# First batch's input on all 128 partitions, a three-product first step, and later raw weights in a Fourier filter with two MLPs

## The chip, the cores and the metric

One core of one Trainium2 chip. TensorE (PE; PEld is its weight load) multiplies, VectorE (DVE), ScalarE (ACT) and GpSimd (POOL) do elementwise work, SyncE (SP) issues most DMAs. The metric is device microseconds (us) of one launch; less is better.

## The reference

```
X = rfft(x, axis=1)                       # x: 2 x 3008 x 256
y = irfft(X * (filt_r + 1j*filt_i)[None], n=3008, axis=1)
t = y.reshape(6016, 256)
h = t @ w_in;  t = (h * sigmoid(h)) @ w_out            # d_ff 2048
g = t @ w_gate; t = (g*sigmoid(g) * (t @ w_val)) @ w_out2   # d_ff 1536
```

All in float32. The kernel makes exact enough products out of pairs of float32r parts (high and low), three products each.

## The kernel before, in words

3008 is 64 x 47, and the transform is done as two short ones by matrix products with constant matrices: step 1 along 47 (padded to 48; two sequences of 48 lie on 96 partitions), step 2 along 64, the filter, step 3 back along 64, step 4 back along 47. The class `Fft` holds one batch (F0, F1).

The fill (lines 1085 to 1230) is written out by hand. F0 is done in full float32. `load_x` brings `x` in eight tiles of 96 partitions x 8 pairs x 128 values; `s1_turned` (line 244) makes four products per four pairs with the `x` values as weights and 96 columns of the constants as the moving side, so that the result is turned, and ACT or DVE copies it into `sc`. `turn` transposes it back, `s2` multiplies by the step 2 matrix and by the filter (`fr`, real part, 64 partitions loaded and `prep_f` writes the negated copy to the other 64; `fi`, imaginary part), `s3` goes back, `store_z` writes to DRAM. `load_zt` reads it back in another layout for `s4`, whose result is split into high and low parts `xh` (ACT, line 377) and `xl` (DVE, line 378): the tokens of the first MLP. `warm` issues products on zeros ahead of the first data. `load_w` brings raw weights, `conv_0` to `conv_c` rework them ("i1" is w_in, "o1" is w_out of the first MLP, in quarters and halves).

From line 1232 on a list of `units` sets the order: one unit is six products of `m1_in` for one token tile and one 128-row group of the hidden layer, and six of `m1_out` of three units earlier. A unit index at which a side task is issued stands in `at(i, ...)`: F1's steps 1 to 4 (in float32r parts), weight conversion, and the `s4` of token tiles 2 to 7 (lines 979 to 984). Units 0 to 31 hold tiles 0 and 1 together, tile 2 begins at unit 32, tile 3 at 48, and so on. All PSUM tiles come from one pool of eight banks; units 0 to 31 keep four of them as accumulators of `m1_out`, and the other four go round among `m1_in`, `s4` and F1's steps. Each engine works its instructions off in the order in which they are written, and SP and ACT issue DMAs in that order too.

Of the kernel before, what the change touches and what calls it, by code (L numbers as in the profile page):

```python
# [14 lines left out]
ALU = mybir.AluOpType  # L15
# [6 lines left out]
N, N1, N2 = 3008, 64, 47  # L22
# [6 lines left out]
P = 128  # L29
# [18 lines left out]


GROUP = 8 * N2  # L50
FW = 576
K4 = ((0, 0, 141), (94, 141, 188), (235, 329, 141))


# [4 lines left out]
def _constants():  # L59

    n1 = np.arange(N1)
    n2 = np.arange(N2)
    k2 = np.arange(SLOT)
    a1 = 2 * np.pi * U1 / N1 * np.outer(n1, n1)
    a2 = 2 * np.pi * V2 / N2 * np.outer(n2, k2)

    c1 = np.zeros((2, NP2, 2, 2, SLOT))
    for p in range(2):
        c1[p, :N2, p, 0] = np.cos(a2)
        c1[p, :N2, p, 1] = -np.sin(a2)  # L70
# [12 lines left out]
    c2[:, 1, 1] = -np.cos(a1)

    c3 = np.zeros((2, N1, N1, 2))
    c3[0, :, :, 0] = np.cos(a1)
    c3[0, :, :, 1] = np.sin(a1)
    c3[1, :, :, 0] = -np.sin(a1)
    c3[1, :, :, 1] = np.cos(a1)
    c3 /= N1  # L90

    k = (E1 * n1[:, None] + E2 * k2[None, :]) % N
    up = k > N // 2
    freq = np.where(up, N - k, k)
    sign = np.where(up, -1.0, 1.0).reshape(N1, 3, 2, 4).transpose(2, 0, 1, 3).reshape(P, 12)
    pack = np.zeros((P, FW + 512), np.float32)
    pack[:96, 0:96] = c1.reshape(96, 96)
    pack[:, 128:256] = c2.reshape(P, P)
    pack[:, 256:384] = c3.reshape(P, P)
    pack[:, 384:396] = sign  # L100
    pack[:, 448:576] = np.eye(P)
    whole = np.kron(np.eye(4), c4.reshape(96, 94))
    for t, (col, o, n) in enumerate(K4):
        pack[:, FW + o:FW + o + n] = whole[P * t:P * t + P, col:col + n]
    return pack, freq
# [6 lines left out]
def fft_filter_mlp_kernel(  # L112
# [13 lines left out]
    nc = tc.nc  # L126
# [35 lines left out]
    c4 = cp.tile([P, 512], F32, name="c4")  # L162
    cst = yp.tile([P, FW], F32, name="cst", bufs=1)

    C1, C2, C3 = (96, 0, 96), (P, 128, 256), (P, 256, 384)
    sgn = cst[:, 384:396]
    eye = cst[:, 448:576]
    csp = yp.tile([P, 2, 384], F32R, name="csp", bufs=1)

    def psum(name):  # L170
# [2 lines left out]
    def mid(shape, name, dtype=F32):  # L173
        return mp.tile(shape, dtype, tag="mid", name=name)
# [11 lines left out]
    PARTS = ((0, 0), (0, 1), (1, 0))  # L186

    def split_consts():
        nc.scalar.copy(csp[:, 0], cst[:, :384])
        nc.vector.tensor_tensor(csp[:, 1], cst[:, :384], csp[:, 0], op=ALU.subtract)  # L190

    def transform(o, m, x):

        k, c0, c1 = m
        if not isinstance(x, tuple):
            nc.tensor.matmul(o, cst[:k, c0:c1], x, start=True, stop=True)
            return
        for i, (mp_, xp_) in enumerate(PARTS):
            nc.tensor.matmul(o, csp[:k, mp_, c0:c1], x[xp_], start=(i == 0), stop=(i == 2))  # L199

    def cut(x, i, j):
        return tuple(v[:, i:j] for v in x) if isinstance(x, tuple) else x[:, i:j]

    class Fft:
# [4 lines left out]
            self.b = b  # L209
            self.xa, self.a, self.ft, self.tin, self.ys, self.zs = {}, {}, {}, {}, {}, {}  # L210

        def load_x(self, i, k=0, n=8):
            if k == 0:
                self.xa[i] = mid([96, 8, P], "x")
            j = 8 * (i % 4) + k
            nc.sync.dma_start(self.xa[i][:, k:k + n], xp[self.b, i // 4, :, j:j + n, :])

        def split(self, x, shape):
            h, l = mid(shape, "fh", F32R), mid(shape, "fl", F32R)
# [24 lines left out]
        def s1_turned(self, i, sc, part=(0, 1)):  # L244

            x = self.xa[i]
            for k in part:
                ps = psum("s1")
                for j in range(4):
                    nc.tensor.matmul(  # L250
                        ps[:, 96 * j:96 * (j + 1)], x[:, 4 * k + j, :], cst[:96, 0:96],
                        start=True, stop=True,
                    )
                m = 32 * (i % 4) + 16 * k
                dst, src = sc[:, :, m:m + 16], ps[:, :384].rearrange("p (m s) -> p s m", s=SLOT)
                if k and i < 4:
                    nc.vector.tensor_copy(dst, src)
                else:
                    nc.scalar.copy(dst, src)
# [15 lines left out]
        def load_f(self, q):  # L275
            self.ft[q] = mid([P, 8, P], "fr"), mid([P, 4, P], "fi")
            f, g = self.ft[q]
            nc.sync.dma_start(f[:64], fr[q])
            nc.sync.dma_start(g, fi[q])

        def prep_f(self, q, part):
            f, o = self.ft[q][0], 4 * part
            nc.scalar.mul(f[64:, o:o + 4], f[:64, o:o + 4], -1.0)

        def prep_g(self, q):
            g, k = self.ft[q][1], 4 * (q % 3)
# [15 lines left out]
        def s2(self, h):  # L302
            q, o = h // 2, 4 * (h % 2)
            (f, g), x = self.ft[q], self.tin[q]
            bps = psum("s2")
            bv = bps.rearrange("p (s d) -> p s d", s=4)
            transform(bv, C2, cut(x, o, o + 4))
            y = yp.tile([P, 4, P], F32, tag="y", name="y")
            t2 = t2t[h % 2]
            nc.vector.tensor_tensor(y, bv, f[:, o:o + 4], op=ALU.mult)  # L310
            for src, dst in ((0, 64), (64, 0)):
                nc.vector.tensor_tensor(  # L312
                    t2[dst:dst + 64], bv[src:src + 64], g[16 * o:16 * o + 64], op=ALU.mult
                )
# [13 lines left out]
        def s3(self, h):  # L328
            q, o = h // 2, 4 * (h % 2)
            y = self.ys.pop(h)  # L330
            zps = psum("s3")
            zv = zps.rearrange("p (s d) -> p s d", s=4)
            transform(zv, C3, y)
            if o == 0:
                self.zs[q] = mid([P, 8, P], "z")
            nc.scalar.copy(self.zs[q][:, o:o + 4], zv)

        def store_z(self, q, o=0, n=8):
            s = 8 * (q % 3) + o
# [48 lines left out]
    def load_w(key, q, half):  # L388


        src = SRC[key]
        raw = mid([P, 512, 2], "raw", U32)
        raws[key, q, half] = raw
        if key in ("o1", "o2"):
            r0 = 512 * q + 256 * half
            nc.sync.dma_start(
                raw.rearrange("p (f d) w -> p f (d w)", f=2),
                src[r0:r0 + 256, :].rearrange("(f p) d -> p f d", p=P),
            )
# [548 lines left out]
    begin = {}  # L948
# [4 lines left out]
    def at(i, fn, *args):  # L953
        todo.setdefault(i, []).append((fn, args))
# [19 lines left out]
    groups, done = [], 0  # L974
# [2 lines left out]
        groups.append([(c, g) for c in range(done, end) for g in range(2)])  # L977
        done = end
    for t in range(2, NSTD):
        i = begin[1, t] - 2 * len(groups[t])  # L980
        for k, (c, g) in enumerate(groups[t]):
            if c % 2 == 0 and g == 0:
                at(i + 2 * k - 5, load_zt, c // 2)
            at(i + 2 * k, s4, c, g)
    def weights2(i, key, q):

        for half in range(2):
# [11 lines left out]
    for b in range(len(WIDE)):  # L999
        i = len(units) + 32 * b  # L1000
# [78 lines left out]
    at(79, fft_s.close)  # L1079
    at(80, room)  # L1080

    WARM = 18
    LAG = 4
    with tc.manual_schedule():
        F0.load_x(0, 0, 4)
        nc.sync.dma_start(cst[:, 0:96], consts[:, 0:96])
        F0.load_x(0, 4, 4)
        nc.vector.memset(idle, 0.0)
        first = stp.tile([P, 512], U32, tag="m", name="m", bufs=4).bitcast(F32)
        nc.vector.memset(first[:, :1], 0.0)  # L1090
        nc.scalar.activation(first[:, :1], first[:, :1], AF.Silu)
        warm(WARM)
        for i in range(1, 4):
            F0.load_x(i)
        nc.sync.dma_start(cst[:, 96:], consts[:, 96:FW])
        F0.load_f(0)
        F0.load_x(4)
        F0.load_f(1)
        F0.load_x(5)
        F0.load_x(6)  # L1100
        F0.load_f(2)
        F0.load_x(7)
        F0.load_f(3)
        nc.sync.dma_start(c4, consts[:, FW:])
        for half in range(2):
            load_w("i1", 0, half)
        for q in range(4, 6):
            F0.load_f(q)
        F1.load_x(0)
        for half in range(2):  # L1110
            load_w("o1", 0, half)
        sc0 = zp.tile([P, SLOT, P], F32, name="sc0")
        sc1 = zp.tile([P, SLOT, P], F32, name="sc1")

# [18 lines left out]

# [169 lines left out]
```

## Time and profile before

| | us |
|---|---|
| three timed runs | 1165.92, 1166.58 (median), 1171.66 |
| the profiled execution | 1170.64 |
| its span | 1168.9 |
| PE busy | 1152.2 (99%) |
| DVE, ACT, POOL busy | 740.1, 670.2, 541.0 |

The profile is of one execution; "idle" is time in which an engine had nothing running, with the one that ended it behind an arrow. The granted clock of TensorE is given as a share of 2.4 GHz, so 0.50 is 1.2 GHz.

### The profile page before, as it was taken

How to read it: one execution, taken by the hardware profiler on the slowest of the kernel's cores; microseconds unless marked ns; L12 is line 12 of the kernel's file. 1: busy time of each engine (PE TensorE's matmuls, PEld its weight loads, DVE VectorE, ACT ScalarE, POOL GpSimd, SP SyncE). 2: the span in 40 equal slices, each digit the busy share in tenths (PEclk: the TensorE clock that was granted, in tenths of full speed). 3: DMA queues.
4: the chain of work that ended last, by engine and by line, in shares of the span. 5: the costliest groups of instructions: out<-in, count | busy, mean ns of one | idle time of the engine just before them, and what ended most of it. 6: DMA issues, size and time to landing. Idle time of an engine off the chain costs nothing.

```text
span 1168.9 us, 16228 instructions
## 1 busy us (share of the span) xinstructions
PE 1152.2 (99%) x6014; PEld 985.9 (84%) x6014; DVE 740.1 (63%) x935; ACT 670.2 (57%) x1095; POOL 541.0 (46%) x370
## 2 busy tenths in 40 slices
PE   9899899999999999999999999999999999999998
PEld 7478688888888888888998888888888888888998
DVE  4678847777666456435356676566666566667555
ACT  4678656667777675656556445445444545444543
POOL 2456624674666466644354343353353353343332
PEclk9999899999999999999999999999999999999999
DMA  9872622443545542511733612412412412413300
GB/s 213 270 230 75 157 75 78 143 136 122 171 164 182 174 165 73 171 54 37 235 116 140 225 41 87 144 55 73 161 41 88 144 56 90 133 49 103 129 17 32
DMA packets 66575, 141.73 MB, mean 121 GB/s; under 512 B 5472, under 2 KB 31072, under 8 KB 66496
## 3 DMA queue, kind: packets, MB, share of 16 engines
q1 hardware_dynamic: 66064, 140.30, 37.1%
q8 instruction: 47, 0.77, 0.3%
q10 hardware_dynamic: 432, 0.39, 0.1%
q14 instruction: 32, 0.26, 0.1%
HBM read 100.56 MB, written 40.11 MB: 120 GB/s over the span
## 4 chain that ended last, share of the span: by engine, by line
PE 75%; issue 1%; DVE 1%; POOL 0%; ACT 0%; DMA 0%; POOLq 0%; ACTq 0%; SPq 0%; DVEq 0%
PE acc L917 17%; PE y L716 15%; PE xa L716 10%; PE xb L716 10%; PE acc L615 8%; PE h L571 7%; PE acc L638 7%; PE s L362 1%; DMA wst<-ds_g 0%; POOL y L316 0%; POOLq L1296 0%; PE s L199 0%; DVE t2t L312 0%; POOL wst L511 0%; DVE xo L690 0%
## 5 line engine op out<-in xcount | busy, mean ns | idle before, releaser
L917 PE MATMUL acc<-w,h 128*128 128x256 f32 x1692 | 433.8, 279 | 0.1
L917 PEld LDWEIGHTS acc<-w,h 128*128 128x128 f32 x1692 | 314.7, 188 | 8.0 <-POOL h L875 0.3
L742 POOL TENSOR_TENSOR s<-s 128x512 f32<-128x512 f32 (+1 forms) x88 | 113.7, 1292 | 265.4 <-ACT s L741 245.4
L615 PE MATMUL acc<-h,w 128*128 128x512 f32 x768 | 200.1, 391 | 0.6 <-DVE h L579 0.6
L579 DVE TENSOR_TENSOR h<-u,h 128x512 fp32r<-128x512 f32 x128 | 135.3, 1063 | 96.8 <-ACT h L578 85.3
L716 PE MATMUL xa<-xo,w 128*128 128x512 f32 (+1 forms) x528 | 193.0, 386 | 0.0
L716 PE MATMUL y<-xo,wst 128*128 128x512 f32 (+1 forms) x528 | 191.0, 387 | 0.1
L716 PE MATMUL xb<-xo,wst 128*128 128x512 f32 (+1 forms) x528 | 190.1, 386 | 0.0
L571 PE MATMUL h<-xh,w 128*128 128x512 f32 x512 | 181.5, 396 | 5.5 <-DVE xl L378 4.9
L615 PEld LDWEIGHTS acc<-h,w 128*128 128x128 f32 x768 | 144.7, 189 | 32.5 <-DVE h L579 2.3
L638 PE MATMUL acc<-h,w 128*128 128x512 f32 (+1 forms) x384 | 138.2, 378 | 0.0
L761 DVE TENSOR_TENSOR c<-y,s 128x512 f32<-128x512 f32 (+1 forms) x88 | 59.5, 676 | 115.6 <-PE y L716 115.6
L900 POOL TENSOR_TENSOR h<-c,h 128x1024 fp32r<-128x1024 f32 (+1 forms) x35 | 83.1, 2373 | 104.4 <-ACT h L899 104.4
L571 PEld LDWEIGHTS h<-xh,w 128*128 128x128 f32 x512 | 96.6, 189 | 26.2 <-DVE xl L378 5.4
L716 PEld LDWEIGHTS y<-xo,wst 128*128 128x128 f32 x528 | 98.9, 187 | 19.0 <-DVE u L748 0.5
L716 PEld LDWEIGHTS xb<-xo,wst 128*128 128x128 f32 x528 | 99.0, 187 | 18.5
L716 PEld LDWEIGHTS xa<-xo,w 128*128 128x128 f32 x528 | 99.0, 188 | 13.8
L598 ACT ACTIVATE u<-h 128x512 f32<-128x512 f32 x128 | 76.2, 596 | 53.9 <-PE h L571 53.4
L571 PE MATMUL h<-xl,w 128*128 128x512 f32 x256 | 100.5, 392 | 0.0
L716 PE MATMUL y<-xo,w 128*128 128x512 f32 (+1 forms) x264 | 97.9, 387 | 0.4 <-DVE c L757 0.4
L872 ACT CAST h<-ga 128x1024 fp32r<-128x1024 f32 (+1 forms) x36 | 37.2, 1034 | 100.9 <-DVE ga L870 100.9
L752 DVE TENSOR_TENSOR xb<-xb,u 128x512 f32<-128x512 f32 (+1 forms) x88 | 60.0, 682 | 43.9 <-PE xb L716 43.9
(122 smaller groups left out, 1829.1 us busy)
## 6 DMA issues: line engine op xcount, KB each, us to landing
wst<-ds_g SPq DMA_DIRECT2D x36, 512.0 KB, 3.5
wst<-ds_v SPq DMA_DIRECT2D x36, 512.0 KB, 3.7
wst<-ds SPq DMA_DIRECT2D x16, 512.0 KB, 4.8
raw<-in_w_out_dram SPq DMA_DIRECT2D x14, 512.0 KB, 5.8
zt<-d SPq DMA_DIRECT2D x16, 384.0 KB, 5.8
x<-in_xp_dram SPq DMA_DIRECT2D x15, 384.0 KB, 9.3
d<-z SPq DMA_DIRECT2D x11, 512.0 KB, 3.9
d<-x SPq DMA_DIRECT2D x20, 256.0 KB, 2.8
```

Source lines behind the costliest of these rows:

```text
L571: nc.tensor.matmul(ps[:, :n], wt[key, f // 4, g][:, wpart, o:o + P], x[xpart][:, g, :n], start=(g == 0 and k == 0), stop=(g == 1 and k == 2),)
L579: nc.vector.tensor_tensor(h[:, 1, :n], u[:, :n], h[:, 0, :n], op=ALU.subtract)
L598: nc.scalar.activation(u[:, :n], ps[:, :n], AF.Silu)
L615: nc.tensor.matmul(a[:, :n], w[:, wpart, o:o + 128], h[:, xpart, :n], start=(f == 0 and k == 0), stop=(f == 15 and k == 2),)
L638: nc.tensor.matmul(a, w[:, wpart, o:o + 128], h[xpart][:, n * l:n * l + n], start=(f == 0 and k == 0), stop=(end and k == 1), skip_group_c ...
L716: nc.tensor.matmul(o, w(wpart), x[:, xpart, :o.shape[-1]], start=(first and k == 0), stop=(last and k == 2), skip_group_check=True,)
L742: nc.gpsimd.tensor_tensor(s[:, 1], s[:, 1], s[:, 0], op=ALU.add)
L752: nc.vector.tensor_tensor(self.b, self.b, self.u2, op=ALU.add)
L761: nc.vector.tensor_tensor(self.c[:, :self.n], self.y, self.s[:, 0], op=ALU.add)
L872: nc.scalar.copy(h[0], a[:, :m])
L900: nc.gpsimd.tensor_tensor(h[1], c, h[0], op=ALU.subtract)
L917: nc.tensor.matmul(a[:, D * (i % 2):D * (i % 2) + D], h[hpart][:, P * i:P * i + P], w[:, wpart, f % 2], start=(at_ == 0 and k == 0 and i % ...
```

## The change

Five things change. (1) F0's `x` tiles are laid out over 128 partitions: of four pairs, the first three stay on 96 partitions, and the fourth is cut into three pieces of 32 rows which go to partitions 96 to 127 beside them (`load_full`). `s1_turned` makes three products per four pairs: two with 144 columns and one with 192, against constants packed to fit; the order of pairs that results is undone by a permuted step 2 matrix (C2T). The 32-row pieces are issued from ACT for tiles 0 to 3 and from SP for tiles 4 to 7. (2) `load_f` loads the first half of `fr` to partitions 0 to 63 and the second half to 64 to 127, two DMAs of 64 rows instead of one; signs follow in `sgn` and in `s3`. (3) The constants come in other pieces: 288 columns first, 320 next, 256 behind `fr`, `fi` of group 1; `c4` comes behind F1's first `x`. (4) The raw weights of `o1` are loaded behind the third store of `z` instead of in the prologue, and `warm` takes 16 products instead of 18. (5) The `s4` calls of tiles 2 to 7 stand at other units: 6, 5, 3 and 2 units ahead of the tile (before: 8, 6, 4, 2), or 5 and 3 where there are two (before: 4, 2).

```diff
-FW = 576
+FW = 896
+ORDER = (0, 3, 2, 1)
...
     def split_consts():
-        nc.scalar.copy(csp[:, 0], cst[:, :384])
-        nc.vector.tensor_tensor(csp[:, 1], cst[:, :384], csp[:, 0], op=ALU.subtract)
+        for i, c, n in ((0, 144, 96), (P, 320, 2 * P)):
+            h, v = csp[:, 0, i:i + n], cst[:, c:c + n]
+            nc.scalar.copy(h, v)
+            nc.vector.tensor_tensor(csp[:, 1, i:i + n], v, h, op=ALU.subtract)
...
+        def load_full(self, i, part=(0, 1), eng=nc.sync):
+
+            if part[0] == 0:
+                self.xa[i] = mid([P, 2, 3, P], "x")
+            x, a, n = self.xa[i], part[0], len(part)
+            j = 8 * (i % 4) + 4 * a
+            src = xp[self.b, i // 4]
+            nc.sync.dma_start(
+                x[:96, a:a + n], src[:, j:j + 4 * n].rearrange("k (a t) e -> k a t e", t=4)[:, :, :3]
+            )
+            for k in part:
+                eng.dma_start(
+                    x[96:, k],
+                    src[:, 8 * (i % 4) + 4 * k + 3].rearrange("(t r) e -> r t e", r=32),
+                )
...
-                for j in range(4):
+                whole = ps[:, 96:480].rearrange("p (b c) -> p b c", c=192)[:, :, :96]
+                both = cst[:, :288].rearrange("p (b c) -> p b c", c=144)[:, :, :96]
+                for n, o, v in (
+                    (0, ps[:, :144], cst[:, 144:288]), (2, ps[:, 144:288], cst[:, 96:240]),
+                    (1, whole, both),
+                ):
                     nc.tensor.matmul(
-                        ps[:, 96 * j:96 * (j + 1)], x[:, 4 * k + j, :], cst[:96, 0:96],
-                        start=True, stop=True,
+                        o, x[:, k, n], v, start=(n == 0), stop=(n == 1), skip_group_check=True
                     )
...
-            nc.sync.dma_start(f[:64], fr[q])
+            for o in range(2):
+                nc.sync.dma_start(f[64 * o:64 * o + 64, 4 * o:4 * o + 4], fr[q][:, 4 * o:4 * o + 4])
             nc.sync.dma_start(g, fi[q])
...
-        i = begin[1, t] - 2 * len(groups[t])
-        for k, (c, g) in enumerate(groups[t]):
+        for n, (c, g) in zip((-6, -5, -3, -2) if len(groups[t]) == 4 else (-5, -3), groups[t]):
             if c % 2 == 0 and g == 0:
-                at(i + 2 * k - 5, load_zt, c // 2)
-            at(i + 2 * k, s4, c, g)
+                at(begin[1, t] + n - 5, load_zt, c // 2)
+            at(begin[1, t] + n, s4, c, g)
...
-    WARM = 18
+    WARM = 16
...
-        nc.sync.dma_start(c4, consts[:, FW:])
...
         F1.load_x(0)
-        for half in range(2):
-            load_w("o1", 0, half)
+        nc.sync.dma_start(c4, consts[:, FW:])
...
                 elif h == 5:
+                    for half in range(2):
+                        load_w("o1", 0, half)
                     for j in range(2):
                         load_zt(j, (0,))
```

SP, in the fill, where the three stores of `z` of F0's first half stand (`d_0_86<-z`), before: the raw weights of `o1` (`in_w_out`) stand ahead of them.

```order
L216 DMA x<-in_xp_dram 96x1024
L396 DMA raw<-in_w_out_dram 128x2x512 x2
L340 DMA d_0_86<-z 128x1024
L216 DMA x<-in_xp_dram 96x1024
L340 DMA d_0_86<-z 128x1024
L216 DMA x<-in_xp_dram 96x1024
L340 DMA d_0_86<-z 128x1024
L353 DMA zt<-d_0_86 128x6x128 x2
```

SP at the same place, of the changed kernel.

```order
L224 DMA x<-in_xp_dram 96x1024
L1141 DMA c_132<-in_consts_dram 128x512
L372 DMA d_0_86<-z 128x1024
L224 DMA x<-in_xp_dram 96x1024
L372 DMA d_0_86<-z 128x1024
L224 DMA x<-in_xp_dram 96x1024
L372 DMA d_0_86<-z 128x1024
L428 DMA raw<-in_w_out_dram 128x2x512 x2
L385 DMA zt<-d_0_86 128x6x128 x2
```

The two raw loads moved from ahead of the first store to between the third store and the read back, and the 256 KB of `c4` took their old place.

PE at the first `s4` of tile 2, before (unit 24; `s_1317` is its PSUM tile, `s_1347` that of F1's step 1 in unit 25).

```order
L362 MATMUL s_1317<-c_132,zt 128x141
L362 MATMUL s_1317<-c_132,zt 128x188
L362 MATMUL s_1317<-c_132,zt 128x141
L571 MATMUL h_1327<-xh,w 128x512
L571 MATMUL h_1327<-xl,w 128x512
L571 MATMUL h_1327<-xh,w 128x512 x2
L571 MATMUL h_1327<-xl,w 128x512
L571 MATMUL h_1327<-xh,w 128x512
L615 MATMUL acc<-h,w 128x512 x6
L199 MATMUL s_1347<-fh,csp 96x512
L199 MATMUL s_1347<-fl,csp 96x512
L199 MATMUL s_1347<-fh,csp 96x512
```

PE at the first `s4` of tile 2, of the changed kernel (units 26 and 27).

```order
L394 MATMUL s_1379<-c_132,zt 128x141
L394 MATMUL s_1379<-c_132,zt 128x188
L394 MATMUL s_1379<-c_132,zt 128x141
L603 MATMUL h_1393<-xh,w 128x512
L603 MATMUL h_1393<-xl,w 128x512
L603 MATMUL h_1393<-xh,w 128x512 x2
L603 MATMUL h_1393<-xl,w 128x512
L603 MATMUL h_1393<-xh,w 128x512
L647 MATMUL acc<-h,w 128x512 x6
L394 MATMUL s_1411<-c_132,zt 128x141
L394 MATMUL s_1411<-c_132,zt 128x188
L394 MATMUL s_1411<-c_132,zt 128x141
```

The first `s4` moved two units later, and the second follows it one unit on instead of two.

DVE at the same place, before: the three instructions of `conv_a` for the last half of `o1` stand between the differences `h` of older units and the `xl` of the first `s4`.

```order
L579 TENSOR_TENSOR h<-u,h 128x512 x2
L423 TENSOR_SCALAR m<-m 128x512
L427 TENSOR_SCALAR m<-m 128x512
L433 SCALAR_TENSOR_TENSOR m<-raw,m 128x512
L378 TENSOR_TENSOR xl<-s_1317,xh 128x376
L579 TENSOR_TENSOR h<-u,h 128x512 x2
L378 TENSOR_TENSOR xl<-s_1378,xh 128x376
```

DVE at the same place, of the changed kernel.

```order
L611 TENSOR_TENSOR h<-u,h 128x512 x2
L455 TENSOR_SCALAR m<-m 128x512
L459 TENSOR_SCALAR m<-m 128x512
L465 SCALAR_TENSOR_TENSOR m<-raw,m 128x512
L611 TENSOR_TENSOR h<-u,h 128x512 x2
L410 TENSOR_TENSOR xl<-s_1379,xh 128x376
L611 TENSOR_TENSOR h<-u,h 128x512
L410 TENSOR_TENSOR xl<-s_1411,xh 128x376
```

Two units' `h` now stand between `conv_a` and the first `xl`.

## Rows read from the trace of the kernel before

**Rows 1.** The page's chain that ended last, by engine

```profile
PE 75%; issue 1%; DVE 1%; POOL 0%; ACT 0%; DMA 0%; POOLq 0%; ACTq 0%; SPq 0%; DVEq 0%
```

**Rows 2.** Waits of PE, whole span: total us, times, longest

```profile
PE h L571 <- DVE xl L378: 4.9, 1, 4.9
PE s L362 <- issue: 3.1, 1, 3.1
PE warm L182 <- DVE m L1090: 1.1, 1, 1.1
```

**Rows 3.** Windows: length, busy of each engine, then PE's clock, DMA share, GB/s

```profile
11.00:27.00 16.00, 15.96 (x110) 12.75 (x109) 11.37 (x17) 8.51 (x16) 7.73 (x7) 1.00 1.04 209
28.00:30.50 2.50, 2.50 (x19) 2.03 (x18) 1.36 (x2) 1.84 (x4) 0.97 (x1) 1.00 1.04 407
40.00:46.00 6.00, 5.72 (x14) 2.36 (x13) 5.29 (x8) 3.95 (x7) 3.54 (x3) 1.00 1.03 398
54.50:57.50 3.00, 3.00 (x9) 1.86 (x8) 1.52 (x4) 1.58 (x4) 0.11 (x1) 0.51 1.02 408
119.00:136.90 17.90, 17.14 (x77) 13.33 (x75) 16.79 (x17) 13.12 (x24) 13.24 (x7) 1.00 0.61 153
141.90:146.90 5.00, 5.00 (x12) 3.94 (x13) 2.04 (x2) 1.74 (x3) 1.03 (x2) 0.52 0.95 259
```

**Rows 4.** Timeline of PE, the first products: start, length

```profile
1.05 4.02 PE L182 MATMUL warm<-idle 128*128 128x256 bf16 x18 [1.05 <-DVE m L1090]
```

**Rows 5.** Timeline of ACT, copies of step 1, every second group

```profile
10.50 0.48 ACT L259 COPY sc<-s 128x384 f32<-128x384 f32 x1 [1.31 <-PE s L250]
...
12.29 0.48 ACT L259 COPY sc<-s 128x384 f32<-128x384 f32 x1 [1.31 <-PE s L250]
```

**Rows 6.** Timeline of PEld, first weights of x tiles 5 and 7

```profile
20.43 0.19 PEld L250 LDWEIGHTS s<-cst,x 96*128 96x128 f32 x1 [0.24 <-DMA x<-in_xp_dram]
...
27.44 0.19 PEld L250 LDWEIGHTS s<-cst,x 96*128 96x128 f32 x1 [0.24 <-ACT sc L259]
```

**Rows 7.** Tile x, the DMA of tile 7: issue and landing

```profile
L216 SPq DMA_DIRECT2D x<-in_xp_dram x1: 312/312/312, 14.6 to 14.6; - x1
...
DMA to landing us min/median/max: 12.3/12.3/12.3
```

**Rows 8.** Tile z, the third store: issue and landing

```profile
L340 SPq DMA_DIRECT2D d<-z x1: 327/327/327, 40.6 to 40.6; - x1
...
DMA to landing us min/median/max: 9.4/9.4/9.4
```

**Rows 9.** Tile zt, the first read back: landing

```profile
DMA to landing us min/median/max: 3.3/3.3/3.3
```

**Rows 10.** Timeline of PE around the first s4

```profile
48.42 1.02 PE L196 MATMUL s<-x,cst 96*96 96x512 f32 x2
49.29 1.02 PE L196 MATMUL s<-y,cst 128*128 128x512 f32 x2
53.39 2.38 PE L362 MATMUL s<-c,zt 128*128 128x141 f32 x12 [3.08 <-issue]
...
59.18 0.48 PE L571 MATMUL h<-xh,w 128*128 128x512 f32 x1
```

**Rows 11.** Timeline of all engines around the first s4 of tile 2

```profile
136.34 0.62 ACT L451 CAST w<-m 128x512 fp32r<-128x512 f32 x1 [1.07 <-POOL m L443]
...
138.35 2.45 POOL L221 TENSOR_TENSOR fl<-x,fh 96x1024 fp32r<-96x1024 f32 x1
138.63 2.72 DVE L433 SCALAR_TENSOR_TENSOR m<-raw,m 128x512 uint32<-128x512 uint32 x1
...
141.27 0.53 DVE L378 TENSOR_TENSOR xl<-s,xh 128x376 fp32r<-128x376 f32 x1
...
141.86 0.79 PE L571 MATMUL h<-xh,w 128*128 128x512 f32 x1 [4.91 <-DVE xl L378]
...
146.95 0.96 PE L362 MATMUL s<-c,zt 128*128 128x141 f32 x6
```

More of the change, by code (lines that the diff above doesn't have):

```diff
@@ L95, in _constants @@
     sign = np.where(up, -1.0, 1.0).reshape(N1, 3, 2, 4).transpose(2, 0, 1, 3).reshape(P, 12)
+    sign[N1:] *= -1
+    c1, c2 = c1.reshape(96, 96), c2.reshape(P, P)
     pack = np.zeros((P, FW + 512), np.float32)
[L97 to L101, printed above, removed]
+    pack[96:, 0:96] = c1[32:64]
+    pack[96:, 96:144] = c1[64:, 48:]
+    pack[:96, 144:240] = c1
+    pack[96:, 240:288] = c1[:32, :48]
+    pack[:, 320:448] = c2
+    pack[:, 448:576] = c3.reshape(P, P)
+    pack[:, 576:704] = c2.reshape(8, 4, 4, P)[:, ORDER].reshape(P, P)
+    pack[:, 704:832] = np.eye(P)
+    pack[:, 832:844] = sign
     whole = np.kron(np.eye(4), c4.reshape(96, 94))
@@ L163, in fft_filter_mlp_kernel @@
     cst = yp.tile([P, FW], F32, name="cst", bufs=1)
-    C1, C2, C3 = (96, 0, 96), (P, 128, 256), (P, 256, 384)
-    sgn = cst[:, 384:396]
-    eye = cst[:, 448:576]
+    C1, C2, C3, C2T = (96, 144, 96, 0), (P, 320, P, 128), (P, 448, P, 256), (P, 576, P, None)
+    sgn = cst[:, 832:844]
+    eye = cst[:, 704:832]
     csp = yp.tile([P, 2, 384], F32R, name="csp", bufs=1)
@@ L188, in split_consts @@
     def split_consts():
-        nc.scalar.copy(csp[:, 0], cst[:, :384])
-        nc.vector.tensor_tensor(csp[:, 1], cst[:, :384], csp[:, 0], op=ALU.subtract)
+        for i, c, n in ((0, 144, 96), (P, 320, 2 * P)):
+            h, v = csp[:, 0, i:i + n], cst[:, c:c + n]
+            nc.scalar.copy(h, v)
+            nc.vector.tensor_tensor(csp[:, 1, i:i + n], v, h, op=ALU.subtract)
     def transform(o, m, x):
-        k, c0, c1 = m
+        k, c, n, r = m
         if not isinstance(x, tuple):
-            nc.tensor.matmul(o, cst[:k, c0:c1], x, start=True, stop=True)
+            nc.tensor.matmul(o, cst[:k, c:c + n], x, start=True, stop=True)
             return
         for i, (mp_, xp_) in enumerate(PARTS):
-            nc.tensor.matmul(o, csp[:k, mp_, c0:c1], x[xp_], start=(i == 0), stop=(i == 2))
+            nc.tensor.matmul(o, csp[:k, mp_, r:r + n], x[xp_], start=(i == 0), stop=(i == 2))
     def cut(x, i, j):
@@ L210, in __init__, with load_x @@
             self.xa, self.a, self.ft, self.tin, self.ys, self.zs = {}, {}, {}, {}, {}, {}
[L212 to L216, printed above, removed]
+        def load_x(self, i):
+            self.xa[i] = mid([96, 8, P], "x")
+            j = 8 * (i % 4)
+            nc.sync.dma_start(self.xa[i], xp[self.b, i // 4, :, j:j + 8, :])
+        def load_full(self, i, part=(0, 1), eng=nc.sync):
[12 more added lines that the diff above has]
+                )
         def split(self, x, shape):
@@ L277, in load_f @@
             f, g = self.ft[q]
-            nc.sync.dma_start(f[:64], fr[q])
+            for o in range(2):
+                nc.sync.dma_start(f[64 * o:64 * o + 64, 4 * o:4 * o + 4], fr[q][:, 4 * o:4 * o + 4])
             nc.sync.dma_start(g, fi[q])
         def prep_f(self, q, part):
-            f, o = self.ft[q][0], 4 * part
-            nc.scalar.mul(f[64:, o:o + 4], f[:64, o:o + 4], -1.0)
+            f, o, a, b = self.ft[q][0], 4 * part, 64 * part, 64 - 64 * part
+            nc.scalar.mul(f[b:b + 64, o:o + 4], f[a:a + 64, o:o + 4], -1.0)
         def prep_g(self, q):
@@ L306, in s2 @@
             bv = bps.rearrange("p (s d) -> p s d", s=4)
-            transform(bv, C2, cut(x, o, o + 4))
+            transform(bv, C2 if self.b else C2T, cut(x, o, o + 4))
             y = yp.tile([P, 4, P], F32, tag="y", name="y")
@@ L335, in s3 @@
                 self.zs[q] = mid([P, 8, P], "z")
-            nc.scalar.copy(self.zs[q][:, o:o + 4], zv)
+            if o:
+                nc.scalar.mul(self.zs[q][:, o:o + 4], zv, -1.0)
+            else:
+                nc.scalar.copy(self.zs[q][:, o:o + 4], zv)
         def store_z(self, q, o=0, n=8):
@@ L1080, in fft_filter_mlp_kernel @@
     at(80, room)
-    WARM = 18
+    WARM = 16
     LAG = 4
     with tc.manual_schedule():
-        F0.load_x(0, 0, 4)
-        nc.sync.dma_start(cst[:, 0:96], consts[:, 0:96])
-        F0.load_x(0, 4, 4)
+        F0.load_full(0, (0,), nc.scalar)
+        nc.sync.dma_start(cst[:, 0:288], consts[:, 0:288])
+        F0.load_full(0, (1,), nc.scalar)
         nc.vector.memset(idle, 0.0)
@@ L1093, in fft_filter_mlp_kernel @@
         for i in range(1, 4):
-            F0.load_x(i)
-        nc.sync.dma_start(cst[:, 96:], consts[:, 96:FW])
+            F0.load_full(i, (0, 1), nc.scalar)
+        nc.sync.dma_start(cst[:, 576:], consts[:, 576:FW])
         F0.load_f(0)
-        F0.load_x(4)
+        F0.load_full(4)
         F0.load_f(1)
-        F0.load_x(5)
-        F0.load_x(6)
+        nc.sync.dma_start(cst[:, 320:576], consts[:, 320:576])
+        F0.load_full(5)
+        F0.load_full(6)
         F0.load_f(2)
-        F0.load_x(7)
+        F0.load_full(7)
         F0.load_f(3)
-        nc.sync.dma_start(c4, consts[:, FW:])
         for half in range(2):
```

## The prediction

> **What bounds the kernel now.** I read the page's chain first, then PE's waits, then the stretches around them. The chain is PE for 75% of the span, and no other engine has over 1% [rows 1]. So a saving counts where PE stands still or where its own work gets shorter, and nearly nowhere else. PE has only two long waits in the whole span, 4.9 us for an `xl` of DVE and 3.1 us in front of the first `s4`; the next one, 1.1 us, is the start of the program [rows 2]. Each of the two is followed by a stretch at half clock, 0.51 and 0.52 of full speed [rows 3], so each costs more than its idle time. The edits touch three places: the fill up to 28 us, the first `s4` at 53.4 us, and tile 2's `s4` from 132 us on.
>
> **Place 1: the fill to 28 us.** Removed: two of 18 products on zeros; 18 take 4.02 us [rows 4], so two are worth 0.45 us. Step 1 has 16 groups of four pairs. Two of ACT's copies, one every second group, start 1.79 us apart, each waiting for PE [rows 5]: a group takes 0.895 us, and at two records for each of its four products a record of 96 columns takes 0.112 us. A record of 512 columns takes 0.435 us (two start 0.87 us apart [rows 10]). The trace has no record of 144 or 192 columns. By columns alone they take 0.122 and 0.163 us, so the new group of 2 x (144, 144, 192) is 0.81 us. Bounds: 0.67 us, if all three ran at 0.112, and 0.9 us, if the wider ones also kept the spare time of the old (0.112 less 0.082 by columns). I take 0.81, since the record of 512 shows that the columns decide for wide ones: 0.085 us less, 1.4 us for 16. With the two products on zeros PE could be 1.8 us earlier.
>
> It can't use most of that, since the data is late next. PE begins x tile 5 with a wait for that tile's DMA [rows 6], and tile 7, issued at 14.6 us, lands 12.3 us later, at 26.9 us [rows 7], when PE gets to it at 27.44 [rows 6]. From 11 to 27 us the DMA share is 1.04 at only 209 GB/s; where tiles of 128 partitions come in one DMA (raw weights, 28 to 30.5 us) the same share moves 407 GB/s [rows 3]. The new layout writes all partitions, but `x` by a DMA of 96 rows and two of 32, and `fr` by two of 64, so the rate lies between these rows, or below, if small pieces hurt; and 147 KB more constants stand ahead of tile 7 (0.7 us at 209 GB/s). I take 260 GB/s, near the lower row: the 3.3 MB of these 16 us take 12.8 us, 3.2 less, or 2.5 with the constants. That would carry PE's 1.8 us. As ACT and PE also wait for `fr` here, of which the same holds, I take 0.7 us as the gain of place 1, with -4 and 1.8 as ends.
>
> ACT now issues eight DMAs of its own, at about 0.32 us each [rows 7, 8] 2.6 us. Its first copy can't be due before 1.05 + 3.57 + 0.81 = 5.4 us [rows 4], which covers them; if an issue took twice as long, the first copies would be up to 2.6 us late, and the eight banks would hold PE's eight groups meanwhile.
>
> The Trainium skill has a rule against this layout: "SBUF — State Buffer", section "Can I just issue two DMAs to hit both halves?", says that two DMAs to the two halves of the partitions run one after the other and gained 6% together in its measurement; only one transfer over all 128 reaches every port. By that rule the rate would stay at 209 GB/s. The trace has no such pair, so it can't say; what the rule makes of the time is the first rival.
>
> **Place 2: the first `s4`.** The wait before it has no name in the profile ("issue"), but the landings give it one. The third store of `z`, issued at 40.6 us, lands 9.4 us later [rows 8], at 50.0, because 1.05 MB of raw weights and two x tiles are ahead of it. The read back goes out then and lands after 3.3 us [rows 9], at 53.3; `s4` starts at 53.39 us [rows 10]. With the raw weights behind the store there is 1.05 MB less ahead of it, 2.6 us at 398 GB/s [rows 3], and PE hands it over 0.7 us earlier: it lands at 46.7 us at best. I take 46.9, and 3.3 us for the read back: 50.2. The raw weights are now ahead of that. They run in the time in which the store's landing is awaited, and I add 0.2 us for their rest (0 to 2.6 at the ends): 50.4 us. PE is there at 50.3 - 0.7 = 49.6. So `s4` starts 3.0 us earlier, after a wait of 0.8 us. Then the clock: from 53.39 to 59.18 us PE works 5.8 us [rows 10], of which three at 0.51 [rows 3], so 1.5 us are lost; without a long pause they come back, less 0.7 us, as the converted weights `w`, which ACT and POOL finish behind the same `s4`, are next in line. Place 2, with place 1 in it: 3.0 + 0.8 = 3.8 us; ends -1 and 6.
>
> The raw weights themselves are first used by the `conv_0` behind the first products of `m1_in_first`, far behind their new landing at about 49 us.
>
> **Place 3: tile 2's first `s4`.** PE stands still for 4.91 us until 141.86, for an `xl` [rows 11]. Four of the eight banks go round; `s4`, its unit's `h` and the two groups of F1's step 1 take them, so the next `h` needs the bank of `s4`, which is free when `xl` has read it. That `xl` is written behind `conv_a`, whose last instruction takes 2.72 us beside a POOL subtraction that ends at 140.8 us [rows 11]. Afterwards 12 products take 141.86 to 146.95 us, 5.09 us [rows 11]; before, 77 took 17.14 us [rows 3], so 12 take 2.67: 2.4 us lost. Together 7.3 us.
>
> In the new order the first `s4` comes two units later, behind two more `h` on DVE. Its bank is now wanted by the second half of the next step 1 in unit 27, after one `h`, one `m1_out`, a second `s4` and half a step 1. When does PE get there? At 0.22 us a product: 136.95 (end of the old step 1), less 0.7 for the `s4` that has left unit 24, 2.7 for unit 25, 0.7 and 2.7 for `s4` and unit 26, 0.7 and 0.7 for the second `s4` and the half step: 143.8 us. What is late next? `conv_a` ends when POOL lets it, 141.35 us; then POOL's add (1.2 us, half of the 2.45 us for twice the elements), ACT's `w` 0.62, `xh` 0.5 (a cast like `w`, of 376 instead of 512), `xl` 0.53 [rows 11]: 144.2 us. With the hand-overs I take a wait of 0.6 us, too short to expect the clock to fall. From unit 25 on DVE has no `conv_a`, and ACT, 13.12 us busy of 17.9 [rows 3], can catch up. Gain 6.7 us, ends 2 and 7.3. For tiles 3 to 7 PE has no long wait before [rows 2] and six banks go round: nothing to gain, 0, with up to 1 us of loss.
>
> Small: six `z` copies with a sign and `split_consts` in two pieces cost ACT and DVE about one more instruction of 0.5 us each, beside PE.
>
> **Sum.** 3.8 + 6.7 = 10.5 us against the profiled execution's 1170.64 us: 1160.1. That one stands 4.1 us over the median of the runs, 1166.58; if none of that lies in the two waits, the result is 1156.0. I put half of it there: **1158 us**.
>
> **Rivals.**
> (1) The halves don't add up, and a 32-row piece goes at half of 209 GB/s: an x tile is then 295 KB at 209 (1.4 us) and 98 KB at 105 (0.9 us), 2.3 instead of 1.9 us. Eight tiles cost 3.5 us and the constants 0.7; tile 7 lands at about 31 us, PE loses that less its own spare 0.5, and the first `s4` starts at about 54 us, no earlier than before. For it: 209 GB/s wherever partial tiles come. Against: many DMAs are queued, and engines that are done with one half can go on to the other. Time: place 2 gives 0 instead of 3.8, the rest as forecast: 1162.
> (2) The wait of place 3 only moves to unit 27: `xl` another 3 us late, as ACT's `w` still stands ahead of `xh`. Half of place 3 stays, 4 us: 1162.
> (3) Slower: DVE is 94% busy ahead of the old pause [rows 3], and the pause let it, ACT and POOL catch up. Without it the debt comes due at the `s4` and F1 steps from unit 27 to 34: four waits of 4.9 us with 2.4 us of half clock each are 29 us, against 10.5 gained: 1177. It decides from the point at which `xl` is over 3 us behind its `s4` twice in a row. Against it: with `conv_a` gone from unit 25 on, DVE has no more than `h`, `xl` and the F1 steps.
>
> **How the numbers follow.** Chances: forecast 0.60 (own range 1153 to 1161.5), (1) 0.14, (2) 0.19, (3) 0.07. The range is 1152 (place 1 at 1.8, hardly a wait at either `s4`, the 4.1 us outside the waits) to 1165 (most of (1) and (2) at once). A change of 0.5%, 5.8 us, is about what a measurement here can tell from none; the border is 1160.8. Faster: 0.6 x 0.9 + 0.14 x 0.3 + 0.19 x 0.4 = 0.66; slower 0.07; within it the rest, 0.27.
>
> **What would show it.** The first `s4` near 50 us, with a wait under 1 us ahead and no half clock behind; the third store landing near 47 us; x tile 7 before 26 us; no wait of PE over 1 us in units 25 to 28, and full clock from 119 to 160 us. It is wrong if x tiles 5 to 7 end waits of PE (1), if PE waits for `xl` in unit 27 (2), or if new waits with half clock stand between 140 and 170 us (3).

## The result, and the profile of the changed kernel

| | before | after |
|---|---|---|
| median of the runs, us | 1167.22 (1165.92 to 1171.66, 4 runs) | 1157.62 (1157.39 to 1158.55, 4 runs) |
| profiled execution, us | 1170.64 | 1157.67 |
| its span, us | 1168.9 | 1155.9 |

The ratio of the times is 0.9913, with a 95% interval from 0.9885 to 0.994. The medians differ by 9.6 us and the two profiled executions by 13.0 us; the experiments below say why these are not the same.

The page's chain by engine, and the waits of PE (total us, times, longest), to be laid beside [rows 1, 2]:

```profile
PE 90%; DVE 3%; ACT 2%; DMA 2%; issue 1%; POOL 1%; POOLq 0%; ACTq 0%; SPq 0%; DVEq 0%
```

```profile
PE warm L189 <- DVE m L1121: 1.1, 1, 1.1
PE s L208 <- POOL fl L245: 0.8, 1, 0.8
PE s L208 <- DVE xl L410: 0.7, 1, 0.7
PE acc L647 <- DVE h L611: 0.6, 3, 0.3
```

Both long waits, 4.9 and 3.1 us, are gone. What is left beside the start of the program is under 1 us each, and one of these, 0.7 us for an `xl`, is new. The windows (columns as in [rows 3]) show full clock in each of the stretches that had half of it:

```profile
11.00:27.00 16.00, 15.96 (x94) 12.20 (x93) 12.11 (x19) 10.05 (x18) 8.14 (x7) 1.00 0.92 265
40.00:46.00 6.00, 5.74 (x13) 1.96 (x11) 5.31 (x8) 3.33 (x7) 3.64 (x3) 1.00 0.98 312
49.00:53.00 4.00, 4.00 (x24) 2.96 (x22) 2.24 (x6) 2.98 (x7) 1.95 (x2) 1.00 0.68 263
137.00:142.00 5.00, 4.31 (x21) 3.21 (x20) 2.56 (x4) 4.09 (x9) 1.58 (x2) 1.00 0.63 225
```

From 11 to 27 us the rate is 265 GB/s, at a DMA share that is down to 0.92, where [rows 3] had 209 at 1.04. Not all of that is x: behind x tile 7 the raw weights come, and from 24.5 to 27 us, with that tile landed, the rate is 313 GB/s.

*Place 1.* ACT's copies of two successive groups of step 1 (timeline of ACT: start, length; before, two copies of every second group [rows 5]), and what one tile's last small pieces of x took to land (source lines of the x loads, 19.5 to 20.3 us):

```profile
18.65 0.48 ACT L287 COPY sc<-s 128x384 f32<-128x384 f32 x1 [0.30 <-PE s L279]
19.47 0.48 ACT L287 COPY sc<-s 128x384 f32<-128x384 f32 x1 [0.34 <-PE s L279]
```

```profile
L237 SPq DMA_DIRECT2D x<-in_xp_dram x2: 423/436/449, 19.6 to 20.1; - x2
...
DMA to landing us min/median/max: 4.1/4.2/4.4
```

A group takes 19.47 - 18.65 = 0.82 us. The last piece of x is there at 20.1 + 4.4 = 24.5 us; before, it was 26.9 [rows 7].

*Place 2.* The third `z` store, the first read back, and PE around the first `s4`:

```profile
L372 SPq DMA_DIRECT2D d<-z x1: 326/326/326, 39.3 to 39.3; - x1
...
DMA to landing us min/median/max: 3.6/3.6/3.6
```

```profile
L385 SPq DMA_DIRECT2D zt<-d x2: 366/452/537, 43.0 to 43.4; - x2
...
DMA to landing us min/median/max: 4.2/4.6/5.0
```

```profile
48.06 1.02 PE L205 MATMUL s<-y,cst 128*128 128x512 f32 x2
48.92 1.77 PE L394 MATMUL s<-c,zt 128*128 128x141 f32 x12
...
52.95 0.49 PE L603 MATMUL h<-xh,w 128*128 128x512 f32 x1
```

The store lands at 39.3 + 3.6 = 42.9 us (before 50.0 [rows 8]), the read back that `s4` needs at 43.0 + 4.2 = 47.2, before PE wants it. `s4` follows the product ahead of it with no wait at 48.92 us (before 53.39 [rows 10]), and the first `h` starts at 52.95, against 59.18.

*Place 3.* The stretch that answers to [rows 11], first DVE, then PE, and PE's first `s4` of before, which [rows 11] leaves out:

```profile
132.81 2.75 DVE L465 SCALAR_TENSOR_TENSOR m<-raw,m 128x512 uint32<-128x512 uint32 x1
135.49 2.37 DVE L611 TENSOR_TENSOR h<-u,h 128x512 fp32r<-128x512 f32 x2
138.36 0.55 DVE L410 TENSOR_TENSOR xl<-s,xh 128x376 fp32r<-128x376 f32 x1 [0.50 <-ACT xh L409]
```

```profile
132.83 0.96 PE L394 MATMUL s<-c,zt 128*128 128x141 f32 x6
...
136.61 0.96 PE L394 MATMUL s<-c,zt 128*128 128x141 f32 x6
...
138.97 0.48 PE L208 MATMUL s<-fh,csp 96*96 96x512 f32 x1 [0.69 <-DVE xl L410]
```

```profile
131.84 0.96 PE L362 MATMUL s<-c,zt 128*128 128x141 f32 x6
```

`conv_a`'s last instruction is as long as before (2.75 us, beside the same POOL copy), and `xl` is behind it as before. What the new units change is where `s4` stands against it. Before, this instruction begins 6.8 us after the first `s4` (138.63 and 131.84), when PE has already wanted the bank since 136.95; now the two begin together (132.81 and 132.83). PE's own work between this `s4` and the next use of its bank is about as long as before, 138.28 - 132.83 = 5.4 us against 5.1. Only the second half of step 1 in unit 27 waits, 0.69 us.

### The profile page after: what moved, and what is told of

It reads as the page before. It is cut to its first block, busy times and chain, and to the rows that moved or that the text cites. A ratio compares the mean times of both kernels' runs of the same rounds, so it can differ in the third digit from the quotient of the medians.

```text
span 1155.9 us, 16231 instructions
## 1 busy us (share of the span) xinstructions
PE 1146.9 (99%) x5980; PEld 981.7 (85%) x5980; DVE 738.3 (64%) x936; ACT 669.7 (58%) x1096; POOL 541.2 (47%) x370
## 4 chain that ended last, share of the span: by engine, by line
PE 90%; DVE 3%; ACT 2%; DMA 2%; issue 1%; POOL 1%; POOLq 0%; ACTq 0%; SPq 0%; DVEq 0%
PE acc L949 17%; PE y L748 15%; PE acc L647 12%; PE h L603 12%; PE xa L748 10%; PE xb L748 10%; PE acc L670 7%; PE s L205 2%; PE s L394 2%; DVE h L611 2%; PE s L208 1%; DMA x<-in_xp_dram 1%; PE s L279 1%; DVE m L455 0%; DVE m L459 0%
```

## The experiments

The change has three parts: the **layout** (x and the real filter on all partitions, and with them the three products, the constants in other pieces and the two products on zeros fewer), the **raws** (the second matrix's raw weights behind the third store) and the **units** (those of tile 2's `s4`, and by the same line of tiles 3 to 7). The medians of each alone, and of each left out, are one table; the paragraphs below say how each came out. The kernel before was run beside every group: its median was 1168.79 us beside the units, layout with raws, and layout with units; 1167.31 beside the raws; 1167.52 beside the layout, and raws with units.

| parts in the kernel | median, us | ratio to before, 95% interval |
|---|---|---|
| raws | 1165.36 | 0.9987 [0.9974, 0.9999] |
| layout | 1165.17 | 0.9976 [0.9961, 0.9991] |
| units | 1160.96 | 0.9935 [0.9917, 0.9952] |
| layout, raws | 1164.34 | 0.9962 [0.9948, 0.9975] |
| raws, units | 1159.22 | 0.9935 [0.9908, 0.9961] |
| layout, units | 1158.30 | 0.991 [0.9893, 0.9927] |

**The old units in the changed kernel.**

```
-        for n, (c, g) in zip((-6, -5, -3, -2) if len(groups[t]) == 4 else (-5, -3), groups[t]):
+        i = begin[1, t] - 2 * len(groups[t])
+        for k, (c, g) in enumerate(groups[t]):
...
```

> The changed kernel with the s4 calls of tiles 2 to 7 back at their old units. Theory (the s4 of tile 2 is written so that its PSUM bank is wanted while DVE is still held in conv_a): PE again waits 4 to 5 us near 130 us in this kernel's time and works some 5 us at half clock behind it; about 7 us more than the changed kernel, near 1164.5 us. Rival (the wait was a late effect of the fill, whose DMAs came late): no wait over 1 us, 1157.5 to 1158.5 us.

Measured: 1164.34 us, 6.7 more than the changed kernel. PE's timeline has the old wait again, to the hundredth:

```profile
130.53 0.40 PE L208 MATMUL s<-fh,csp 96*96 96x512 f32 x1
135.84 0.80 PE L603 MATMUL h<-xh,w 128*128 128x512 f32 x1 [4.91 <-DVE xl L410]
```

So place 3 is made by the units alone and not by what the fill does to later work.

**The new units alone**, in the kernel before (the same lines, the other way).

> The kernel before with the new units of the s4 calls alone. Theory: the 4.9 us wait and the half clock behind it go, as in the changed kernel, and the fill stays: 6.5 to 7 us less than before, 1160 to 1161 us, with a wait of about 0.7 us at unit 27. Rival (the wait only moves when the fill is not shortened too): a wait of 3 us or more at unit 27, 1164 us or more.

Measured: 1160.96 us, 7.8 less than the 1168.79 beside it. In this kernel PE's waits end so:

```profile
52.95 3.47 PE L362 MATMUL s<-c,zt 128*128 128x141 f32 x12 [2.19 <-issue]
...
144.61 0.47 PE L199 MATMUL s<-fh,csp 96*96 96x512 f32 x1 [0.72 <-DVE xl L378]
```

Place 2's wait is still there (this execution, 1163.66 us, is the slowest of six), place 3's has shrunk from 4.9 to 0.7 us. So what the units gain does not hang on the fill.

**Why DVE is late there**, in the kernel before: the POOL subtraction `fl`, and with it ACT's cast `fh` (which stands behind `xh` there anyway), goes one unit later, so that `fl` no longer runs beside the end of `conv_a`.

```
-        at(i - 1, F1.split_x, k)
+        at(i if k == 7 else i - 1, F1.split_x, k)
```

> The kernel before with the POOL copy fl of the last block's first-stage split issued one unit later, so that it no longer runs beside the last instruction of conv_a on DVE. If DVE's late end at tile 2's s4 is made by that POOL copy: the DVE instruction that took 2.72 us takes under 1.5, the 4.91 us wait for xl falls to 2 to 3.5 us, 1162 to 1166 us. Rival (only the order of the s4 pieces and their shared buffers make the wait): the wait stays 4.5 to 5 us, 1167 to 1169 us.

Measured: 1165.54 us, ratio 0.9985 [0.9971, 0.9999]. On DVE, ACT and PE:

```profile
133.37 0.69 DVE L433 SCALAR_TENSOR_TENSOR m<-raw,m 128x512 uint32<-128x512 uint32 x1
133.98 0.54 DVE L378 TENSOR_TENSOR xl<-s,xh 128x376 fp32r<-128x376 f32 x1
```

```profile
131.60 0.46 ACT L377 CAST xh<-s 128x376 fp32r<-128x376 f32 x1
```

```profile
134.57 0.61 PE L571 MATMUL h<-xh,w 128*128 128x512 f32 x1 [2.90 <-DVE xl L378]
```

The instruction falls from 2.72 to 0.69 us and the wait from 4.91 to 2.90. So 2.0 us of the wait were the POOL subtraction. The other 2.9 us are the order on DVE: `xh` is ready at 132.06 us, but `xl` stands behind `conv_a` and begins at 133.98. In the changed kernel `conv_a` is as slow as before, and the new order alone takes the wait to 0.69 us.

**The raws back in the prologue**, in the changed kernel.

```
+        for half in range(2):
+            load_w("o1", 0, half)
...
-                    for half in range(2):
-                        load_w("o1", 0, half)
```

> The changed kernel with the raw weights of o1 loaded in the prologue again, behind c4. Theory as forecast (the 1.05 MB of raw weights ahead of the third store are what held the read back): the store lands about 3 us later than in the changed kernel (46 us instead of 42.9), the read back near 50.5, s4 waits about 1.5 us; 1159 to 1161 us. Rival (the faster loads ahead of it alone did it, the place of the raw weights does not matter): s4 starts without a wait, as in the changed kernel, 1157.5 to 1158 us.

Measured: 1158.30 us, 0.7 more, between the two ranges. The store lands 6.2 us after its issue, where the changed kernel has 3.6: at 45.9 us, as the theory has it. But the read back then takes 3.4 us, and `s4` still starts with next to no pause (PE's timeline):

```profile
48.45 1.02 PE L205 MATMUL s<-y,cst 128*128 128x512 f32 x2
49.46 1.84 PE L394 MATMUL s<-c,zt 128*128 128x141 f32 x12
```

So the raws do hold the store up, by 3.0 us, and with the layout in place nearly all of that passes while PE is still busy.

**The raws alone**, in the kernel before (the same two lines moved).

> The kernel before with one part of the change: the second matrix's raw weights are issued behind the third z store instead of in the prologue. Forecast's theory (the raws are what the store and its read back queue behind): the third store lands 3 to 4 us earlier, the s4 of tile 0 starts with a wait under 1 us, its first product at 49.5 to 50.5 us instead of 53.39; about 1163 to 1165 us against 1167 to 1169. Rival (the backlog is the slow x and filter loads, the raws only ride on it): a wait of 2 us or more stays ahead of s4, start after 52 us, 1166 us or more.

Measured: 1165.36 us. The store (its source line, then its landing) and PE:

```profile
L340 SPq DMA_DIRECT2D d<-z x1: 327/327/327, 40.0 to 40.0; - x1
...
DMA to landing us min/median/max: 3.2/3.2/3.2
```

```profile
48.77 1.02 PE L196 MATMUL s<-y,cst 128*128 128x512 f32 x2
49.63 1.77 PE L362 MATMUL s<-c,zt 128*128 128x141 f32 x12
```

There is no wait in this trace: the forecast's mechanism is there, and its start of `s4` (49.5 to 50.5 us) too. The store lands at 43.2 us, 6.8 us before that of the first trace of before, where 3 to 4 were expected. But the time is just over the upper edge of what was expected, 2 us below the median of before, and one of the eleven runs took 1171.55 us. That opened a question: the profiled execution of before lost over 4 us at this place, and its median can't have.

**The kernel before, profiled twice more.**

> The kernel before, unchanged, for a second profiled execution: its timed runs spread over 6 us (1165.4 to 1171.6). Theory: the wait of 3.1 us ahead of tile 0's s4 and the half clock behind it belong to executions in which the fill's transfers are slow (209 GB/s at 11 to 27 us); an execution near 1165.5 us shows 230 GB/s or more there and a wait under 1 us, one of 1169 us or more the wait of 2 to 3 us; the 4.9 us wait at tile 2's s4 is in both. Rival: the wait ahead of tile 0's s4 is 3 us in every execution and the spread comes from elsewhere.

> As before_again1, a third profiled execution: by the theory the time follows the wait ahead of tile 0's s4 (0 to 3.1 us, plus up to 2 us of half clock) and the rate at 11 to 27 us; by the rival neither follows the time.

Measured: 1169.18 and 1165.49 us. PE at the first `s4`, in the slower and then in the faster one:

```profile
52.22 2.87 PE L362 MATMUL s<-c,zt 128*128 128x141 f32 x12 [2.25 <-issue]
```

```profile
50.61 1.77 PE L362 MATMUL s<-c,zt 128*128 128x141 f32 x12
```

With the first trace of before there are three executions: 1170.64, 1169.18 and 1165.49 us have waits of 3.1, 2.2 and 0 us there; the store takes 9.4, 7.9 and 5.9 us to land; the rate from 11 to 27 us is 209, 212 and 225 GB/s (230 or more was expected of the last). The wait of 4.9 us is in all three. Two kernels above have the same fill, and their traces go the same way: the units alone with 202 GB/s, 8.5 us and a wait of 2.2 us, and the one with the later `fl` with 245 GB/s, 6.2 us and no wait:

```profile
49.53 1.84 PE L362 MATMUL s<-c,zt 128*128 128x141 f32 x12
```

So what tells these executions of before apart, up to 5.2 us, is mostly this one wait and its half clock (4.5 us at the first `h`: 59.18 and 54.64), and the first trace came from the late end. The four runs of the changed kernel lie within 1.2 us.

**The layout alone** (raws and units as before).

> The kernel before with the new layout of x and of the filter alone; the raw weights stay in the prologue and the s4 units are the old ones. Theory (the layout as well as the raws' place takes the transfers out of the way): no wait over 1 us ahead of tile 0's s4, 4.9 us at tile 2's s4, 1164.3 to 1165.5 us. Rival (the raws' place is what counts): a wait of 2 us or more ahead of tile 0's s4, 1167 us or more.

Measured: 1165.17 us, and `s4` starts without a wait:

```profile
49.17 1.79 PE L394 MATMUL s<-c,zt 128*128 128x141 f32 x12
```

One trace without the wait does not show that the layout removes it, since two of the five traces of the old fill have none either; nor does the one of the raws. The times say more: eleven of the twelve runs lie between 1163.75 and 1165.71 us, with one at 1168.77, while those of before beside them go from 1164.93 to 1173.01. Whether the two gains add up stays open. The raws alone bring 2.0 us (1167.31 less 1165.36), the layout alone 2.4 (1167.52 less 1165.17); both together 4.5 with the old units (1168.79 less 1164.34), but 3.3 with the new (1160.96 less 1157.62), and the medians of before differ by 1.5 us between the groups.

**Raws and units, without the layout.**

> The kernel before with two parts of the change, the raw weights behind the third store and the new units of s4, without the new layout of x and of the filter. If the parts add up: 1165.3 (raws alone) less 6.7 (what the old units cost in the changed kernel), 1158.6 us; the layout is then worth about 1 us (0.8 in the fill's products). Rival (the layout is needed for the loads to be on time): a wait of 1 us or more ahead of tile 0's s4 or in the fill, 1160 us or more.

Measured: 1159.22 us median, so these two parts add up to within 0.6 us, and the layout is worth about 1.6. But one of its six runs, the profiled one, took 1165.39 us, and not at place 2. PE's timeline of the fill:

```profile
6.35 1.13 PE L250 MATMUL s<-cst,x 96*128 96x96 f32 x8 [0.68 <-DMA x<-in_xp_dram]
7.79 10.55 PE L250 MATMUL s<-cst,x 96*128 96x96 f32 x48 [0.31 <-DMA x<-in_xp_dram]
```

```profile
8.00:20.00 12.00, 12.00 (x57) 11.68 (x58) 1.75 (x4) 1.44 (x3) 1.06 (x2) 0.50 1.05 207
```

The 48 records that take 5.6 us at full clock take 10.55 here, at a granted clock of 0.50 from 8 to 20 us (the window's columns are those of [rows 3]).

**x on 96 partitions** in the changed kernel, by one load a tile; the four products and the order of the constants go back with it, the filter stays halved.

```
+                self.xa[i] = mid([96, 8, P], "x")
...
+            nc.sync.dma_start(self.xa[i][:, k:k + n], xp[self.b, i // 4, :, j:j + n, :])
```

> The changed kernel with F0's x tiles on 96 partitions in one DMA each and four products per four pairs, as before; fr in halves, raw weights and s4 units as changed. Theory (layout over 128 partitions raises the DMA rate and shortens PE's work): from 11 to 27 us about 220 GB/s instead of 265, x tiles 5 to 7 just in time or late, PE 1.3 us longer in step 1, s4 later by 1.5 to 3 us: 1159 to 1161 us. Rival, by the rule that two DMAs to two halves don't add up (the Trainium skill, SBUF - State Buffer): the rate is not changed by the layout of x, 265 GB/s stays, and only PE's 1.3 us come back: 1159 us at most.

**The filter on 64 rows in one load** in the changed kernel; x stays on 128.

```
-            for o in range(2):
-                nc.sync.dma_start(f[64 * o:64 * o + 64, 4 * o:4 * o + 4], fr[q][:, 4 * o:4 * o + 4])
+            nc.sync.dma_start(f[:64], fr[q])
...
```

> The changed kernel with the real filter again in one load of 64 rows (the signs' constants as before); x stays on 128 partitions. If the filter's halves carry part of the higher rate: 11 to 27 us falls from 265 GB/s to 210 to 235, filter pieces land 7 us or more after issue instead of 3.8, PE gets waits for them of 0.5 to 2 us, 1158.5 to 1160 us. Rival (x's layout alone carries it): rate 250 or more, 1157.5 to 1158.

**One load of 128 partitions for an x tile**, from an input that the host has laid out so.

```
...
+            nc.sync.dma_start(self.xa[i][:, a:a + n], xf[i, :, a:a + n])
```

> The changed kernel with x laid out by the host so that each tile is one load to 128 partitions instead of two of 96 and 32. If two loads to parts of the partitions do not add up to a full one: the rate at 4 to 12 us rises by 20 percent or more and the 0.6 us that PE waits for the second tile goes, 1157.0 to 1157.4 us. Rival (they add up): rate in the same stretch within 10 percent, waits unchanged, 1157.6 us. In both PE bounds the rest, so the time moves by 0.7 us at most.

Measured: 1158.67, 1157.61 and 1157.32 us. The windows (columns as above) from 11 to 27 us, in that order, with those from 4 to 12 us of the first and the last, and then that of the changed kernel:

```profile
4.00:12.00 8.00, 7.44 (x65) 7.09 (x62) 1.67 (x3) 1.69 (x4) 0.00 (x0) 1.00 0.99 240
11.00:27.00 16.00, 15.96 (x107) 12.49 (x106) 11.49 (x18) 9.53 (x18) 8.06 (x7) 1.00 1.05 227
```

```profile
11.00:27.00 16.00, 15.96 (x94) 12.20 (x94) 12.08 (x19) 9.45 (x18) 8.12 (x7) 1.00 1.07 257
```

```profile
4.00:12.00 8.00, 7.57 (x52) 6.90 (x50) 1.67 (x3) 1.91 (x4) 0.00 (x0) 1.00 1.03 328
11.00:27.00 16.00, 15.96 (x94) 12.20 (x94) 12.11 (x19) 10.39 (x19) 8.12 (x7) 1.00 1.06 302
```

```profile
4.00:12.00 8.00, 7.85 (x50) 7.30 (x48) 1.67 (x3) 1.65 (x4) 0.00 (x0) 1.00 0.91 240
```

How much of the rate is the layout's can't be read from one trace of each. From 11 to 27 us the traces with x on 96 rows have 198 to 245 GB/s (eight), those with 96 and 32 rows 250 to 265 (five), and part of the difference is the raw weights that come behind a tile 7 that lands sooner. From 4 to 12 us, ahead of them, there is none: 228 to 263 and 228 to 251 GB/s. What is left is tile 7's landing, at 24.3 to 25.6 us with the two loads and at 25.7 to 27.9 without (seven traces, without that at half clock). With x on 96 rows `s4` starts at 49.58 us, 0.7 later than in the changed kernel and not 1.5 to 3, and four of the six runs are at 1158.2 to 1158.8 us, under the 1159 to 1161 expected.

The filter's halves carry next to none of the rate (257) and none of the time: the expectation of a loss was wrong. One load of 128 partitions moves 328 GB/s from 4 to 12 us, 37% above what 96 and 32 rows reach together, and lands tile 7 at 21.5 us, so here the expectation that the two do not add up came true, except that a wait of PE for x of 0.4 us stayed. Yet it brings 0.3 us, which is inside the spread: PE is busy for 15.96 of the 16 us from 11 to 27 in all of these, and has nothing to gain from a load that comes still earlier.

## Why the prediction was right

**Place 1** was right in size. A group takes 0.82 us (forecast 0.81), the two products on zeros 4.02 - 3.59 = 0.43 us (0.45), and the rate from 11 to 27 us is 265 GB/s (taken 260), though that number holds raw weights too. PE reaches the last product before the first `s4` 1.2 us earlier (49.29 to 48.06), and 1.0 us on the average of the traces with the old fill (48.59 to 49.75, six) and the new (47.93 to 48.45, five), where 0.7 were taken and 1.8 was the bound. Rival (1) falls: tile 7 landed at 24.5 us and not at 31, and x never held up PE from tile 2 on.

Rival (1) came out of a rule of the Trainium skill ("SBUF — State Buffer", "Can I just issue two DMAs to hit both halves?"): two loads to the two halves of the partitions serialize and gain 6%, and only one transfer over all 128 reaches every port. The traces go with it further than the forecast did: from 4 to 12 us one load moves 328 GB/s, and the two of 96 and 32 rows 240, which is no more than one of 96 rows. What was wrong was the price that rival (1) put on it.

**Place 2** was right in its direction and mis-sized: 3.8 us forecast, 59.18 - 52.95 = 6.2 us between the two profiled executions. The step that failed is "it lands at 46.7 us at best"; the store landed at 42.9 us. What the raws cost was sized well: 2.6 us forecast, and with the layout in place the store takes 6.2 us to land with the raws ahead of it and 3.6 with them behind. What the forecast took as given is the rest of the 9.4 us. In the five traces of the old fill with the raws ahead the store takes 5.9 to 9.4 us, so up to 3.5 us of it belonged to that one execution. In the seven traces with the raws behind it takes 2.9 to 3.8 us, with either layout. And the forecast put the gain on the raws; the layout alone brings about as much time, though the store still takes 6.0 us there.

**Place 3** was right step by step: 6.7 us forecast, 6.1 to 7.8 measured in the four pairs of kernels that differ in the units alone; the new wait forecast in unit 27 at 0.6 us, 0.69 measured, at the bank of the first `s4` and for its `xl`, without half clock behind (1.00 from 119 to 160 us). From the end of `conv_a`, PE came 2.7 us later (forecast 2.4) and the end of `xl` 3.4 (2.9, to which hand-overs were added). Rival (2), by which half of the old wait would come back in unit 27, falls by the size of the new one: that PE waits for `xl` there, its sign in the prediction, was also forecast. Rival (3), by which a debt of the side engines would come due from there on, falls too; PE has no wait over 0.3 us after it.

**The sum** came out by two errors that cancel. The forecast subtracted 10.5 us from the late profiled execution, where 13.0 was right, and then took off 2.1 us, for the half of that execution's distance to the median that it put outside the two waits. The two further traces show that the distance is mostly the wait at place 2 itself; without the 2.1 us the same sum would have given 1160.1. That the two errors are of one size is luck. By the medians layout and raws together are worth 3.3 us and the units 7.8, or 4.5 and 6.7, in the order in which they are put in; that is 11.2 from the 1168.79 us of that group, while the medians of the result, from 1167.22, differ by 9.6. Two sums that carried nothing are off: the upper bound of a group at place 1 comes to 1.0 us if all six records keep the spare time, and rival (3)'s 29 us on top of the forecast to 1187 and not 1177.

## What to carry to other kernels

A wait that hangs on a backlog of transfers can differ from run to run (here 0 to 3.1 us): before a sum is made from one profiled execution, see where that execution stands among the runs, and ask whether the wait is the difference. Where two edits relieve the same queue, a trace without the wait is no proof for either, if the kernel without them has such traces too; compare many runs. And where an engine is late at one point, the work that needs it can be moved to a place where the engine is free: here two units later, with about as much of PE's work in between as before.

## What the runs showed of the hardware that was not expected

The clock fell behind pauses of 2.2 to 4.9 us in every trace that had them, and behind none of the single ones of 0.5 to 1.0 us. But in the fill, where PE waited for x twice within 2 us, one execution (0.68 and 0.31 us) went to half clock until about 21 us, and another of the same start (before, third trace: 1.01 and 0.33 us) stayed at full clock, as did three traces with the new layout (0.19 to 0.53 us). What tells them apart stays open. The kernel with x on 96 partitions had two runs in six at 1165 us; neither was profiled, but the mean granted clock of their spans was 0.993, where the other four had 1.00 and the execution above 0.994. So they too ran at a lower clock somewhere; where was not seen. None of the 20 runs with the new units and x on 128 partitions was over 1159.2 us.
